# Output copies and x splits put in another order at block ends, and ten conversion steps put later, in a fused attention, ELU and gated kernel

## The chip, the cores and the metric

One core of a Trainium2 chip runs the whole program. Five engines work beside one another, each through its own queue in order: TensorE (PE in the profile; PEld is its weight load), VectorE (DVE), ScalarE (ACT), GpSimd (POOL) and the queue of SyncE (SP), which issues all DMAs of this kernel. The metric is the device time of one execution in microseconds; lower is better.

## What is computed

The reference is a chunked softmax attention whose output feeds two feed-forward layers, cut here to what matters:

```python
# q, k, v: (8, 8, 576, 64), chunks of 64
attn = softmax(q_c @ k_c.T / 8)             # per chunk, rows of 64
x = (attn @ v_c) as (4608, 512)             # tokens x model
h = x @ w_in                                # 512 -> 2048
x = where(h > 0, h, exp(min(h, 0)) - 1) @ w_out      # 2048 -> 512
gate = 1 / (1 + exp(-(x @ w_gate)))         # 512 -> 1536
out = (gate * (x @ w_val)) @ w_out2         # 1536 -> 512
```

## The kernel before, in words

**Precision.** Weights arrive as 64-bit floats and are turned into fp32 on the chip. Every large product is three matmuls in fp32r: each operand is cut into a high part (a cast) and a low part (the fp32 value minus the high part), and high x high, low x high and high x low are added (`PASSES`, lines 33 and 188). A low part of x or of the activations g is a subtraction on VectorE or, for some chunks of x, on GpSimd (`split`, lines 94 to 96; `split_x`, line 182). The profile shows all these subtractions under line 96 and the casts under line 90, except for block 0, where they stand at lines 423 and 664.

**Blocks and slots.** The 4608 tokens are nine blocks of 512. A block's first layer pair is 16 slots, one for each 128 of the 2048 inner columns. Slot s is number f = s mod 16 of block j = s div 16 and runs on TensorE, in this order: some attention work of the next block, `layer_1(s)` (12 matmuls into `h`, lines 425 to 431 and 189; the input x is four chunks of 128 rows, `xs0` to `xs3`, with one buffer each), and `layer_2(s-2)` (12 matmuls into four output banks `y0` to `y3`, line 441, again one buffer each). The ELU of a slot is spread over the next: ScalarE takes exp (`elu_exp`, line 405) and relu (408), VectorE one fused sum (`elu_sum`, 411), ScalarE the cast (`elu_split`), VectorE the low part (`elu_low`, 423; in later blocks line 96).

**Attention of later blocks.** Even slots start with the scores of a pair of chunks (line 280), odd slots with the product with v (`values`, line 379). From pair 10 on (slot 18), q and k are split in odd slots (lines 248 to 258), and the probabilities are turned by small DMAs (line 346) and split (lines 92, 96, 357) in the next even slot.

**Block ends.** Before slot f = 0 of a new block can run `layer_1`, its x chunks must be split; before slot f = 2 can run `layer_2` for the new block, the finished `y0` to `y3` must be copied out (`y_out`, lines 449 to 459: even banks by ScalarE, odd ones by VectorE, each into a tile of the pool `e`, then a DMA to memory).

**Block 0** has no block before it to hide its attention. `first_block` (lines 555 to 664) runs eight pairs through all engines; in its last rounds (the drain) it finishes x chunk by chunk. The weights of the first layer pair are converted at the same time: `convert` (line 106) makes a list of 162 small steps, five for each of 32 weight tiles: a sign, a clamp, an add, a shift and a subtraction on VectorE (lines 140, 134, 146, 137, 155), three of them with an operation on ScalarE beside it (a cast, line 90, and lines 128 and 124); the add also issues the DMA that loads a later tile (line 118). `bg(n)` puts the next n steps of the list at its place in the code. `PRE_STEPS` says how many each round of `first_block` takes, the other tables how many each slot takes.

The order on each engine is the order of the code (`manual_schedule`); waits follow from the data and the buffers.

Of the kernel before, what the change touches and what calls it, by code (L numbers as in the profile page):

```python
# [8 lines left out]
F32 = mybir.dt.float32  # L9
# [8 lines left out]
CH = 64  # L18
# [5 lines left out]
NB = NT // TB  # L24
# [15 lines left out]
EARLY, EARLY_LAG = 2, 5  # L40


PRE_STEPS = (0, 0, 3, 3, 2, 2, 2, 2, 2, 2, 4, 4, 4)
FIRST_STEPS, A0_STEPS, A8_STEPS, B_STEPS = 3, 9, 6, 9

W_AT = (1, 2, 4, 6)

# [5 lines left out]
def kernel(  # L53
# [27 lines left out]
    w_p = ctx.enter_context(tc.tile_pool(name="w", bufs=2 * F1))  # L81
    x_p = ctx.enter_context(tc.tile_pool(name="x", bufs=1))
    g_p = ctx.enter_context(tc.tile_pool(name="g", bufs=2))
    e_p = ctx.enter_context(tc.tile_pool(name="e", bufs=3))
    ps_y = ctx.enter_context(tc.tile_pool(name="ps_y", bufs=1, space=bass.MemoryType.PSUM))
    ps_h = ctx.enter_context(tc.tile_pool(name="ps_h", bufs=2, space=bass.MemoryType.PSUM))

# [94 lines left out]
    def split_x(key, kk, lo_eng):  # L182
        x = xs[key, kk] = x_p.tile([128, 2, TB], F32R, tag=f"xs{kk}", name=f"xs{kk}")
        split(xr.pop((key, kk)), x[:, 0], x[:, 1], nc.scalar, lo_eng)
# [18 lines left out]
    def phase_a():  # L203
        with (
# [87 lines left out]

            def first_parts(P, what):

                t = st[P, what + "1"] = s_p[0].tile([128, 4, CH], F32, tag="s1", name="s1", bufs=2)
                for a, p in enumerate(halves):
                    nc.scalar.copy(out=t[p], in_=parts_of(st[P, what], p, a)[0])  # L297

# [36 lines left out]

            def blocks_out(P):

                d = s_p[0].tile([128, 2, 4, 32], F32, tag="dt", name="dt", bufs=2)
                nc.vector.transpose(
                    out=d.rearrange("p b n q -> p n b q"),  # L340
                    in_=st.pop((P, "p")).rearrange("p n (b k) -> p n b k", b=2),
                )
                t = st[P, "tt"] = s_p[0].tile([64, 4, 128], F32, tag="tt", name="tt", bufs=2)
                for b in range(2):
                    for w in range(4):
                        nc.sync.dma_start(
                            out=t[32 * b:32 * b + 32, w],
                            in_=d[32 * w:32 * w + 32, b].rearrange("p n q -> p (n q)"),
                        )
# [99 lines left out]
            def y_out(j, es=range(KC)):  # L449
                for e in es:  # L450
                    if j == NB - 2:
                        y = xr_tile("y", e)
                    else:
                        y = e_p.tile([128, TB], F32, tag="e", name="y")
                    if e % 2 == 0:
                        nc.scalar.copy(out=y, in_=y_t.pop((j, e)))  # L456
                    else:
                        nc.vector.tensor_copy(out=y, in_=y_t.pop((j, e)))
                    nc.sync.dma_start(out=ymid[j][:, e], in_=y)

            def slot(s, steps=0):
# [9 lines left out]
                def is_pair(n, least=0):  # L471
                    return least <= n < NP
# [8 lines left out]
                else:  # L481
# [3 lines left out]
                        first_parts(V, "v")  # L485
                    elif is_pair(V):
                        values_out(V)
                if f == 0 and j > 0:
                    split_x(j, KC - 1, nc.vector)
                if s >= F1:  # L490
                    elu_sum(s - 1)
                if even and is_pair(P):
# [17 lines left out]
                    elu_sum(s - 1)  # L510
                if s >= EARLY:
                    layer_1(s, 2)
                if f == 2 and j > 0:
                    y_out(j - 1, (2, 3))
                if s == F1 - 1:

                    layer_1(s, 3)
                    transposes(T)
                    transposes_out(T)
                if last:  # L520
                    split_x(nxt, 0, nc.gpsimd)
                bg(q[1])
                layer_1(s)
                if s > 0:
                    elu_split(s - 1)
                if even and 0 <= P < P32:
                    softmax_exp(P)
                if last:
                    split_x(nxt, 1, nc.vector)
                now = not even and 0 <= T < P32 and s >= F1  # L530
                if now:
                    transposes(T)
                elu_exp(s)
                if now:
                    transposes_out(T)
                if even and PB <= P < P32:
# [2 lines left out]
                if 0 < s <= F1:  # L539
                    elu_low(s - 1)  # L540
                elu_rest(s)
                if last:
                    split_x(nxt, 2, nc.gpsimd)
                bg(q[3])
                if even and is_pair(P) and P < PB:
                    softmax_sum(P)
                if s >= 2:
                    layer_2(s - 2)
                if not even and is_pair(T) and s < F1 - 1:
                    transposes(T)  # L550
                    transposes_out(T)
                if f == 1 and j > 0:
                    y_out(j - 1, (0, 1))

            def first_block(load_w):

# [109 lines left out]
            with (  # L666
                tc.tile_pool(name="conv0", bufs=2) as conv_p,
                tc.tile_pool(name="ps_0", bufs=2, space=bass.MemoryType.PSUM) as ps_p[0],
            ):
                make_identity(nc, ident)  # L670
                tiles = [(k, w_src[k[0]][k[1]], w_p) for k in w1]
                first_block(convert(tiles, conv_p, len(W_AT), 6))
                for s in range(F1):
                    slot(s, A0_STEPS if s else FIRST_STEPS)
                bg(len(todo))
            with (
                tc.tile_pool(name="att2", bufs=1) as s_p[0],
# [7 lines left out]
    def phase_b(slot, layer_2, elu_sum, elu_split, y_out):  # L685
        with (
# [2 lines left out]
            tc.tile_pool(name="ps_b", bufs=2, space=bass.MemoryType.PSUM) as ps_b,  # L689
        ):  # L690
            tiles = [(k, w_src[k[0]][k[1]], w_p if n < 2 * F1 else w2_p) for n, k in enumerate(w2)]
            load_w = convert(tiles, conv_p, 4, 4)
            for n in range(4):
                load_w(n)
            for s in range((NB - 1) * F1, NB * F1):
                slot(s, A8_STEPS if s < NB * F1 - 1 else 0)
# [157 lines left out]
```

## Time and profile before

| | |
|---|---|
| three timed runs | 1807.86, 1809.66, 1810.4 us; median 1809.66 |
| the profiled execution | 1808.78 us, of which the span from the first to the last instruction is 1807.0 |
| TensorE busy | 1776.1 us (98%), mean granted clock 0.997 |
| VectorE, ScalarE, GpSimd busy | 1044.9 (58%), 757.1 (42%), 44.2 (2%) |

A busy TensorE is one with a matmul under way; matmuls overlap, so a steady stream shows no idle time. The timeline gives each group of equal instructions its start, its length and, in brackets, the idle time of its engine before it with the instruction that ended it. The span has three parts: block 0 with its attention (0 to some 141 us), the slots of blocks 1 to 8 (to some 918 us) and the gated layers.

### The profile page before, as it was taken

How to read it: one execution, taken by the hardware profiler on the slowest of the kernel's cores; microseconds unless marked ns; L12 is line 12 of the kernel's file. 1: busy time of each engine (PE TensorE's matmuls, PEld its weight loads, DVE VectorE, ACT ScalarE, POOL GpSimd, SP SyncE). 2: the span in 40 equal slices, each digit the busy share in tenths (PEclk: the TensorE clock that was granted, in tenths of full speed). 3: DMA queues.
4: the chain of work that ended last, by engine and by line, in shares of the span. 5: the costliest groups of instructions: out<-in, count | busy, mean ns of one | idle time of the engine just before them, and what ended most of it. 6: DMA issues, size and time to landing. Idle time of an engine off the chain costs nothing.

```text
span 1807.0 us, 21535 instructions
## 1 busy us (share of the span) xinstructions
PE 1776.1 (98%) x8068; PEld 1471.1 (81%) x8068; DVE 1044.9 (58%) x1980; ACT 757.1 (42%) x1411; POOL 44.2 (2%) x50
## 2 busy tenths in 40 slices
PE   7999999999999999999999999999999999999999
PEld 6887878788888878788888888888888888888887
DVE  7997888888888888887767423222222222222322
ACT  7775666767666766767654201010110101010101
POOL 1000000000000000000000000000000000000000
PEclk9999999999999999999999999999999999999999
DMA  6652121121212122215343101000010101010000
GB/s 231 200 169 77 57 80 59 58 69 53 74 57 82 48 79 59 69 47 166 117 128 106 47 1 47 1 24 24 9 38 0 47 0 48 1 47 1 24 1 24
DMA packets 61593, 111.52 MB, mean 62 GB/s; under 512 B 11056, under 2 KB 30000, under 8 KB 61488
## 3 DMA queue, kind: packets, MB, share of 16 engines
q1 hardware_dynamic: 61488, 110.14, 19.3%
q8 instruction: 63, 1.03, 0.2%
q14 instruction: 42, 0.34, 0.1%
HBM read 84.15 MB, written 18.87 MB: 57 GB/s over the span
## 4 chain that ended last, share of the span: by engine, by line
PE 83%; DVE 9%; ACT 5%; issue 1%; DMA 1%; SPq 0%; POOL 0%; DVEq 0%
PE o L730 16%; PE pv L189 16%; PE pg L189 16%; PE y L441 16%; PE h L189 15%; PE banks L379 1%; PE banks L280 1%; ACT pt L357 1%; DVE t L140 1%; DVE elu L411 1%; DVE s L310 1%; DVE w L155 1%; DVE xs L96 1%; DVE qv L258 1%; DVE t L146 1%
## 5 line engine op out<-in xcount | busy, mean ns | idle before, releaser
L189 PE MATMUL h<-xs,w 128*128 128x512 f32 x1728 | 426.3, 394 | 5.7 <-DVE xs L96 3.9
L441 PE MATMUL y<-g,w 128*128 128x512 f32 x1728 | 419.5, 391 | 8.3 <-ACT y L456 7.6
L719 DVE TENSOR_TENSOR sg<-pv,sg 128x512 f32<-128x512 f32 x108 | 74.6, 691 | 548.6 <-PE pv L189 545.6
L441 PEld LDWEIGHTS y<-g,w 128*128 128x128 f32 x1728 | 323.2, 188 | 80.2 <-ACT y L456 10.1
L189 PEld LDWEIGHTS h<-xs,w 128*128 128x128 f32 x1728 | 317.1, 189 | 69.0 <-DVE xs L96 6.4
L714 ACT ACTIVATE sg<-pg 128x512 f32<-128x512 f32 x108 | 64.5, 597 | 676.9 <-PE pg L189 676.6
L189 PE MATMUL pv<-xs,w 128*128 128x512 f32 x1296 | 311.3, 389 | 0.0
L189 PE MATMUL pg<-xs,w 128*128 128x512 f32 x1296 | 311.3, 389 | 0.0
L730 PE MATMUL o<-w,g 128*128 128x512 f32 x1296 | 311.1, 389 | 0.0
L189 PEld LDWEIGHTS pv<-xs,w 128*128 128x128 f32 x1296 | 243.2, 188 | 50.5
L189 PEld LDWEIGHTS pg<-xs,w 128*128 128x128 f32 x1296 | 243.2, 188 | 50.5
L730 PEld LDWEIGHTS o<-w,g 128*128 128x128 f32 x1296 | 243.2, 188 | 50.5
L411 DVE SCALAR_TENSOR_TENSOR elu<-h,elu 128x512 f32<-128x512 f32 x144 | 99.4, 690 | 65.5 <-ACT elu L408 64.2
L405 ACT ACTIVATE elu<-h 128x512 f32<-128x512 f32 x144 | 86.0, 597 | 53.6 <-PE h L189 25.6
L297 ACT COPY s<-banks 64x256 f32<-64x256 f32 x216 | 78.2, 362 | 67.5 <-PE banks L280 64.3
L90 ACT CAST g<-elu 128x512 fp32r<-128x512 f32 x144 | 89.3, 620 | 23.0 <-DVE elu L411 18.5
L408 ACT ACTIVATE elu<-elu 128x512 f32<-128x512 f32 x144 | 90.9, 631 | 3.8
L96 DVE TENSOR_TENSOR g<-elu,g 128x512 fp32r<-128x512 f32 x128 | 87.9, 686 | 6.3 <-ACT g L90 4.6
L96 DVE TENSOR_TENSOR g<-sg,g 128x512 fp32r<-128x512 f32 x108 | 74.9, 694 | 3.7
L96 POOL TENSOR_TENSOR xs<-xr,xs 128x512 fp32r<-128x512 f32 x26 | 36.8, 1417 | 1631.1 <-ACT xs L90 1631.1
L315 ACT ACTIVATE e<-s 128x256 f32<-128x256 f32 x64 | 26.8, 418 | 111.2 <-DVE s L312 110.7
L357 ACT CAST pt<-pt 64x512 fp32r<-64x512 f32 x108 | 66.8, 619 | 4.5 <-DVE pt L92 2.2
(86 smaller groups left out, 1299.2 us busy)
## 6 DMA issues: line engine op xcount, KB each, us to landing
raw<-in_qkv SPq DMA_DIRECT2D x54, 512.0 KB, 3.7
wraw<-in_w_out SPq DMA_DIRECT2D x28, 512.0 KB, 3.5
xr<-ymid SPq DMA_DIRECT2D x36, 256.0 KB, 3.6
wraw<-in_w_in SPq DMA_DIRECT2D x16, 512.0 KB, 3.7
ymid<-y SPq DMA_DIRECT2D x32, 256.0 KB, 3.1
out<-o SPq DMA_DIRECT2D x32, 256.0 KB, 2.0
tt<-dt SPq DMA_DIRECT2D x432, 16.0 KB, 1.8
wraw<-in_w_gate SPq DMA_DIRECT2D x12, 512.0 KB, 3.6
```

Source lines behind the costliest of these rows:

```text
L90: nc.scalar.copy(out=out, in_=raw)
L96: lo_eng.tensor_sub(out=lo, in0=raw, in1=hi)
L189: nc.tensor.matmul(out=ps, lhsT=w[:, zw, kk * 128:(kk + 1) * 128], rhs=xs[key, kk][:, zx], start=(kk == 0 and n == 0), stop=(kk == KC - 1 ...
L297: nc.scalar.copy(out=t[p], in_=parts_of(st[P, what], p, a)[0])
L357: nc.scalar.copy(out=t[h1, z], in_=t[h0, z])
L405: nc.scalar.activation(out=e_t[s], in_=h_t[s], func=ACTF.Exp)
L408: nc.scalar.activation(out=e_t[s], in_=e_t[s], func=ACTF.Relu, scale=-1.0, bias=1.0)
L411: nc.vector.scalar_tensor_tensor(out=e_t[s], in0=h_t.pop(s), scalar=0.0, in1=e_t[s], op0=ALU.max, op1=ALU.subtract,)
L441: nc.tensor.matmul(out=y_t[j, e], lhsT=w[:, zw, e * 128:(e + 1) * 128], rhs=g[:, zx], start=(f == 0 and n == 0), stop=(f == F1 - 1 and n = ...
L714: nc.scalar.activation(out=sg, in_=pg, func=ACTF.Sigmoid)
L719: nc.vector.tensor_tensor(out=sg, in0=pv, in1=sg, op=ALU.mult)
L730: nc.tensor.matmul(out=o_t[t], lhsT=g[:, zx, t * 128:(t + 1) * 128], rhs=w[:, zw], start=(f == 0 and n == 0), stop=(f == F2 - 1 and n == 2),)
```

## The change

It does the following.

- **Block ends, x.** All four chunks of the next block are split in the last slot of a block, right behind `layer_1`, the low parts all on VectorE. Before, chunk 0 stood ahead of the end of `layer_1` and chunk 2 behind the relu, both with the low part on GpSimd; chunk 1 stood behind the cast of the ELU and chunk 3 in the first slot of the next block, both on VectorE.
- **Block ends, y.** All four copies stand at the end of slot f = 1. Before, banks 0 and 1 stood there, banks 2 and 3 in slot f = 2.
- **Buffers.** The pool `e` has 5 buffers instead of 3; the tiles `s1`, `dt` and `tt` of the attention have one instead of two; in the second conversion three weight tiles are loaded ahead instead of four.
- **Conversion steps.** The rounds 8 to 12 of `first_block` take 8 steps instead of 16. Slot 0 takes 4 instead of 3, slot 1 takes 5 instead of 9, slots 2 to 15 take 10 instead of 9 until the 162 are done.
- **Pair 1's turned probabilities** move from the end of slot 1 into slot 2, behind `layer_1`.

```diff
-PRE_STEPS = (0, 0, 3, 3, 2, 2, 2, 2, 2, 2, 4, 4, 4)
-FIRST_STEPS, A0_STEPS, A8_STEPS, B_STEPS = 3, 9, 6, 9
+PRE_STEPS = (0, 0, 3, 3, 2, 2, 2, 2, 1, 1, 2, 2, 2)
+FIRST_STEPS, A0_STEPS, A8_STEPS, B_STEPS = 4, 10, 6, 9
...
-    e_p = ctx.enter_context(tc.tile_pool(name="e", bufs=3))
+    e_p = ctx.enter_context(tc.tile_pool(name="e", bufs=5))
...
-                if f == 0 and j > 0:
-                    split_x(j, KC - 1, nc.vector)
                 if s >= F1:
                     elu_sum(s - 1)
...
                 if s >= EARLY:
                     layer_1(s, 2)
-                if f == 2 and j > 0:
-                    y_out(j - 1, (2, 3))
...
-                if last:
-                    split_x(nxt, 0, nc.gpsimd)
                 bg(q[1])
                 layer_1(s)
+                if last:
+                    for kk in range(KC if j + 1 < NB else KC - 1):
+                        split_x(nxt, kk, nc.vector)
+                if s == 2:
+                    transposes(1)
                 if s > 0:
                     elu_split(s - 1)
                 if even and 0 <= P < P32:
                     softmax_exp(P)
-                if last:
-                    split_x(nxt, 1, nc.vector)
...
                 elu_exp(s)
+                if s == 2:
+                    transposes_out(1)
...
                 elu_rest(s)
-                if last:
-                    split_x(nxt, 2, nc.gpsimd)
                 bg(q[3])
...
-                if not even and is_pair(T) and s < F1 - 1:
+                if not even and is_pair(T) and 1 < s < F1 - 1:
...
                 if f == 1 and j > 0:
-                    y_out(j - 1, (0, 1))
+                    y_out(j - 1)
...
-                    slot(s, A0_STEPS if s else FIRST_STEPS)
+                    slot(s, FIRST_STEPS + s if s < 2 else A0_STEPS)
...
-            load_w = convert(tiles, conv_p, 4, 4)
-            for n in range(4):
+            load_w = convert(tiles, conv_p, 3, 4)
+            for n in range(3):
                 load_w(n)
```

**ScalarE in slot 31, the last of block 1** (`xs0` to `xs3` are block 2's x, `g` and `elu` the ELU of slots 30 and 31). Before:

```order
L255 CAST qv_2402<-raw_2321 64x2x256
L90 CAST xs0_2415<-xr0_1557 128x512
L90 CAST g_2424<-elu_2375 128x512
L90 CAST xs1_2427<-xr1_1807 128x512
L405 ACTIVATE elu_2430<-h_2408 128x512
L408 ACTIVATE elu_2430<-elu_2430 128x512
L90 CAST xs2_2433<-xr2_2044 128x512
L297 COPY s1_2454<-banks_1499 64x256 x2
L90 CAST xs3_2457<-xr3_2281 128x512
```

Now:

```order
L255 CAST qv_2402<-raw_2321 64x2x256
L90 CAST xs0_2421<-xr0_1557 128x512
L90 CAST xs1_2424<-xr1_1807 128x512
L90 CAST xs2_2427<-xr2_2044 128x512
L90 CAST xs3_2430<-xr3_2281 128x512
L90 CAST g_2433<-elu_2375 128x512
L405 ACTIVATE elu_2436<-h_2408 128x512
L408 ACTIVATE elu_2436<-elu_2436 128x512
```

The four high parts stand together ahead of the ELU's cast, exp and relu; on VectorE the four low parts stand together in the same way, between line 258 and the ELU's low part.

**VectorE over the end of slot 33 and slot 34** (`y1` and `y3` are finished banks of block 1; the rows from line 310 to 339 are the softmax of a pair, `g` the ELU's low parts). Before:

```order
L458 COPY y_2573<-y1_1668 128x512
L411 SCALAR_TENSOR_TENSOR elu_2555<-h_2539,elu_2555 128x512
L310 TENSOR_TENSOR s_2586<-banks_1499,s1_2582 64x256 x2
L311 TENSOR_REDUCE m_2587<-s_2586 128x4
L312 TENSOR_TENSOR s_2586<-s_2586,m_2587 128x256
L92 CAST pt_2593<-tt_2480 64x512
L96 TENSOR_TENSOR pt_2593<-tt_2480,pt_2593 64x512
L319 TENSOR_REDUCE d_2598<-e4_93 128x4
L320 RECIPROCAL d_2598<-d_2598 128x4
L322 TENSOR_TENSOR p_2601<-e4_93,d_2598 128x256
L339 STREAM_TRANSPOSE dt_2603<-p_2601 128x4x2x32
L458 COPY y_2624<-y3_1670 128x512
```

Now:

```order
L96 TENSOR_TENSOR g_2552<-elu_2505,g_2552 128x512
L458 COPY y_2573<-y1_1668 128x512
L458 COPY y_2579<-y3_1670 128x512
L411 SCALAR_TENSOR_TENSOR elu_2555<-h_2539,elu_2555 128x512
L310 TENSOR_TENSOR s_2592<-banks_1502,s1_2588 64x256 x2
```

The copy of `y3` moved from behind the softmax of slot 34 to ahead of it; on ScalarE the copy of `y2` moved likewise, from behind lines 315 and 357.

**ScalarE in the last rounds of block 0's drain** (`w`, `wraw` and `t` from `wraw` are conversion steps; `xs3` is the last chunk of block 0's x). Before:

```order
L90 CAST xs2_389<-xr2_363 128x512
L90 CAST w_391<-t_234 128x512
L128 ACTIVATE wraw_211<-wraw_211 128x512
L648 COPY zeros_104<-ps_t_394 64x2x128 x2
L654 COPY xr3_419<-bank_397 64x256 x2
L124 ACTIVATE t_422<-wraw_271 128x512
L90 CAST w_436<-t_294 128x512
L128 ACTIVATE wraw_271<-wraw_271 128x512
L654 COPY xr3_419<-bank_427 64x256 x2
L90 CAST xs3_443<-xr3_419 128x512
```

Now:

```order
L124 ACTIVATE t_387<-wraw_211 128x512
L645 COPY zeros_104<-ps_t_390 64x2x128 x2
L651 COPY xr3_404<-bank_393 64x256 x2
L90 CAST w_407<-t_234 128x512
L128 ACTIVATE wraw_211<-wraw_211 128x512
L651 COPY xr3_404<-bank_411 64x256 x2
L90 CAST xs3_431<-xr3_404 128x512
```

Between the fourth last round and the high part of `xs3`, six conversion operations (one of them just ahead of the rows shown) became three.

## Rows read from the trace of the kernel before

**Rows 1.** The page, part 1: busy time, share, instructions

```profile
PE 1776.1 (98%) x8068; PEld 1471.1 (81%) x8068; DVE 1044.9 (58%) x1980; ACT 757.1 (42%) x1411; POOL 44.2 (2%) x50
```

**Rows 2.** Waits, whole span: who waited for whom, us in total, times, longest

```profile
ACT elu L405 <- DMA ymid<-y: 15.2, 6, 2.7
...
PE y L441 <- ACT y L456: 7.6, 6, 1.3
...
PE h L189 <- DVE xs L96: 3.9, 6, 0.7
```

**Rows 3.** Timeline, TensorE, blocks 1 to 2: start, length, what [idle before <-releaser]

```profile
227.82 0.63 PE L280 MATMUL banks<-kz,qv 128*128 128x256 f32 x4
...
239.70 0.65 PE L280 MATMUL banks<-kz,qv 128*128 128x256 f32 x4
...
242.15 1.88 PE L189 MATMUL h<-xs,w 128*128 128x512 f32 x7 [0.64 <-DVE xs L96]
...
246.88 0.75 PE L379 MATMUL banks<-pt,qv 128*128 128x256 f32 x4
...
252.92 0.63 PE L280 MATMUL banks<-kz,qv 128*128 128x256 f32 x4
...
258.94 1.91 PE L441 MATMUL y<-g,w 128*128 128x512 f32 x6 [1.30 <-ACT y L456]
...
266.63 0.63 PE L280 MATMUL banks<-kz,qv 128*128 128x256 f32 x4
...
278.63 0.63 PE L280 MATMUL banks<-kz,qv 128*128 128x256 f32 x4
```

**Rows 4.** Timeline, the other engines, same stretch

```profile
236.65 0.62 ACT L90 CAST xs<-xr 128x512 fp32r<-128x512 f32 x1
...
237.41 1.71 POOL L96 TENSOR_TENSOR xs<-xr,xs 128x512 fp32r<-128x512 f32 x1 [92.71 <-ACT xs L90]
...
238.00 1.67 DVE L258 TENSOR_TENSOR qv<-raw,qv 64x512 fp32r<-64x512 f32 x1
...
240.31 2.38 DVE L96 TENSOR_TENSOR xs<-xr,xs 128x512 fp32r<-128x512 f32 x2
...
242.72 0.69 DVE L411 SCALAR_TENSOR_TENSOR elu<-h,elu 128x512 f32<-128x512 f32 x1
...
252.53 0.57 ACT L456 COPY y<-y 128x512 f32<-128x512 f32 x1
...
258.30 0.59 ACT L456 COPY y<-y 128x512 f32<-128x512 f32 x1
```

**Rows 5.** Windows, start of program: busy by engine, TensorE clock, DMA share, GB/s

```profile
35.00:40.00 5.00, 3.77 (x17) 2.60 (x15) 3.63 (x7) 4.87 (x11) 0.00 (x0) 1.00 0.35 105
...
45.00:50.00 5.00, 5.00 (x18) 3.94 (x18) 4.93 (x12) 4.55 (x10) 0.00 (x0) 0.50 0.77 247
```

**Rows 6.** Windows, VectorE alone, two slots of block 0

```profile
68.00:81.00 13.00, 12.90 (x28) 1.00 0.67 204
```

**Rows 7.** Timeline, block 0 and its end, all engines

```profile
40.14 0.62 ACT L90 CAST xs<-xr 128x512 fp32r<-128x512 f32 x1
...
42.30 0.69 DVE L664 TENSOR_TENSOR xs<-xr,xs 128x512 fp32r<-128x512 f32 x1
...
50.25 0.69 DVE L423 TENSOR_TENSOR g<-elu,g 128x512 fp32r<-128x512 f32 x1
...
136.51 0.69 DVE L423 TENSOR_TENSOR g<-elu,g 128x512 fp32r<-128x512 f32 x1
...
138.41 2.90 PE L441 MATMUL y<-g,w 128*128 128x512 f32 x12
...
144.75 1.19 PE L189 MATMUL h<-xs,w 128*128 128x512 f32 x4 [0.62 <-POOL xs L96]
...
145.77 2.90 PE L441 MATMUL y<-g,w 128*128 128x512 f32 x12
...
161.24 0.96 PE L441 MATMUL y<-g,w 128*128 128x512 f32 x3 [0.66 <-DVE y L458]
```

More of the change, by code (lines that the diff above doesn't have):

```diff
@@ L293, in first_parts @@
             def first_parts(P, what):
-                t = st[P, what + "1"] = s_p[0].tile([128, 4, CH], F32, tag="s1", name="s1", bufs=2)
+                t = st[P, what + "1"] = s_p[0].tile([128, 4, CH], F32, tag="s1", name="s1")
                 for a, p in enumerate(halves):
@@ L336, in blocks_out @@
             def blocks_out(P):
-                d = s_p[0].tile([128, 2, 4, 32], F32, tag="dt", name="dt", bufs=2)
+                d = s_p[0].tile([128, 2, 4, 32], F32, tag="dt", name="dt")
                 nc.vector.transpose(
@@ L342, in blocks_out @@
                 )
-                t = st[P, "tt"] = s_p[0].tile([64, 4, 128], F32, tag="tt", name="tt", bufs=2)
+                t = st[P, "tt"] = s_p[0].tile([64, 4, 128], F32, tag="tt", name="tt")
                 for b in range(2):
```

## The prediction

> **What bounds the kernel now.** I read the page's busy times first: TensorE is busy 1776.1 of 1807.0 us [rows 1], so no more than some 31 us of waiting can go. About 11 of these lie in the first 45 us, where block 0 has nothing to overlap with; the table of waits tells where the rest is. TensorE waits six times for a low part of x on VectorE and six times for a copy of a finished output bank on ScalarE [rows 2]: once each at six block ends. The timeline of one of them gives the true price, since matmuls overlap and the bracket understates a stop. The score matmuls of even slots are a clock that strikes every two slots: 227.82 to 239.70 is an undisturbed stretch, 11.88 us; the next three take 13.22, 13.71 and 12.00 [rows 3]. So one block end costs 1.34 + 1.83 + 0.12 = 3.29 us, and the six from block 1 to block 7 cost 19.7. The end of block 0 is a seventh, with its own waits (0.62 and 0.66 in brackets [rows 7]); after block 7 TensorE does not stop.
>
> Block 0's slots are the other place to read. There VectorE is busy 12.90 of the 13 us that two slots take [rows 6], and TensorE never stops either: two engines at their limit at once. The low part of slot 13's ELU ends at 136.51 + 0.69 = 137.20, and the matmuls that need it start at 138.41 [rows 7]. VectorE is only 1.2 us ahead.
>
> **The x splits at a block end.** The first stop has a cause that the timeline shows. GpSimd's subtraction runs from 237.41 for 1.71 us, and beside it line 258 on VectorE takes 1.67 us; two chunks of x, beside GpSimd's next one, take 2.38 [rows 4], where one operation of that length alone takes 0.69 (the ELU's sum at 242.72 [rows 4]). So GpSimd costs VectorE about 0.98 + 1.0 us, and chunk 1, caught behind it, is what the matmul at 242.15 waited for [rows 3]. The Trainium skill, "SBUF — State Buffer", section "Who interferes with whom", calls this an exclusive lock for two-input VectorE operations against a reading GpSimd operation; line 258 ends 0.55 us after GpSimd, which fits a blocked start better than a slow run. By that rule alone up to both GpSimd operations, some 3.1 us, would return to VectorE instead of 2.0, and the wait of 0.35 us left below would go too, 2 us over six ends.
>
> Now all four low parts are VectorE's. In slot 31 ScalarE begins the high parts at 236.65 as before [rows 4]; four at 0.62 end near 239.1, the last not held up, since `layer_1(31)` is through chunk 3 about 237. Line 258 starts at 238.00 and, alone, ends at 238.7; four low parts at no more than 0.69 end by 241.4. TensorE has its scores at 239.70 [rows 3] and starts `layer_1(32)` half a microsecond later; a matmul takes (11.88 - 1.0)/48 = 0.227 us (48 in two slots, beside 1.0 us of attention), so chunk 3's low part, for the twelfth matmul, is wanted at 240.2 + 11 x 0.227 = 242.7. It is there. What is late next: behind the four on VectorE stand the ELU's low part (to 242.0, wanted by `layer_2(30)` at 242.9) and the ELU's sum, which starts near 241.9 instead of 242.72. The softmax and the split probabilities hang on that sum; before, they let `values` start at 246.88 [rows 3], now 0.85 earlier, at 246.0. TensorE comes there at 240.2 + 24 x 0.227 = 245.65. It waits 0.35, and the stretch takes 12.35 us instead of 13.22.
>
> **The y copies.** Before, `y2` is copied at 258.30, behind the softmax of slot 34 [rows 4], and the matmuls into that bank start at 258.94 after 1.30 us of idleness [rows 3]. Now it follows `y0`, whose copy ran at 252.53 [rows 4], 0.87 earlier by the shift above: `y0` 251.7, `y2` 252.3, on VectorE `y1` 252.5 and `y3` to 253.9. `layer_2(32)` now wants them at 252.05 + 0.47 + 2.73 = 255.25, so 1.4 us of room hide them. The five buffers make four copies at once possible. Two things are queued behind: VectorE's sum, softmax and split probabilities of slot 34 are 0.6 later by one copy and 0.87 earlier by the shift, ready at 257.9 for a TensorE at 258.0; and the split of q and k in slot 35, which I place at 263.8, against scores wanted at 263.9. Both just make it, so the stretch takes 11.9 instead of 13.71. On SP the next raw load stands behind four output DMAs, so it issues near 255 for a use at 260, with several microseconds of DMA between. The next stretch loses its 0.12, since exp no longer waits for an output DMA (15.2 us in six waits on ScalarE [rows 2]).
>
> Sum for one end: 38.93 us of three stretches become 12.35 + 11.9 + 11.88 = 36.13, **2.8 us saved, 16.8 for six**. Bounds: all of the 3.29 (19.7), or only the y part, 1.95 (11.7), if VectorE's longer row costs at `values` or at the scores what it saves at x.
>
> **The moved conversion steps.** In the drain ScalarE is the limit: from 35 to 40 us it is busy 4.87 of 5, VectorE 3.63 [rows 5]. Three of its conversion operations, at about 0.6, now stand behind the high part of chunk 3, not ahead (40.14 [rows 7]), so this comes at 38.4; the low part, which at 42.30 [rows 7] stood behind steps that waited for ScalarE, follows at 39.0, **3.3 us earlier**. By the queue order, slot 0's ELU then has its low part at about 47.0 instead of 50.25 [rows 7]. It has ten steps fewer ahead of it; at 0.49 us each (28 instructions in 13 us are 0.46, and steps are three long and two short in five; an estimate from [rows 6]) that is 4.9 us of work gone for 3.25 us gained, so VectorE idles 1.6 us more in the drain. The steps are not gone: up to slot 13's low part there are 129 behind that point instead of 117. VectorE was full over that way (136.51 - 50.25 = 86.26 us [rows 7]) and needs 12 x 0.49 = 5.9 more. It gets there at 47.0 + 86.26 + 5.9 = 139.1, and TensorE's `layer_2(13)` starts at 139.85, not 138.41: **1.4 us later**, the head start eaten by waits for VectorE over the slots. Loads move with their add steps, by at most a slot on a lightly used SP; the weights themselves are ready a slot ahead of their use.
>
> At the end of block 0 the four low parts follow in time, so the way from `layer_2(13)` to `layer_2(14)`, 145.77 - 138.41 = 7.36 us with the stop at 144.75 [rows 7], becomes 6.27: 146.1, 0.35 later. The wait for a y copy at 161.24 [rows 7] goes, with what it cost, 0.9. Block 0 and its end: **0.5 us saved**. Bounds: 5 saved, if VectorE does not bind; 2 lost, if each moved step costs 0.6 and the drain idles more.
>
> The smaller buffers and pair 1's moved transposes I take at nothing: each reader is ahead of the next writer on the same engine or a slot away. Three weight tiles ahead instead of four leaves a load six steps of time; it is covered by the slack of the gated slots, where TensorE never waits.
>
> The profiled execution: 1808.78 - 16.8 - 0.5 = **1791.5 us**. It lies 0.9 below the median of the runs, within their spread.
>
> **Rivals.** (1) *VectorE's longer row at a block end moves the stop.* For it: my margins at `values` and at the scores are 0.1 us or negative. Against: GpSimd's interference goes. Then 1.95 per end: 1808.8 - 11.7 - 0.5 = 1796.6. (2) *VectorE does not bind in block 0*, its steps packing closer than 0.49: the 3.3 us stay, with both stops at the block end, so 5: 1808.8 - 16.8 - 5 = 1787. Against it: 12.90 of 13. (3) *Slower: TensorE's clock falls in block 0.* Before, it was granted 0.50 from 45 to 50 us, after a drain in which TensorE was busy 3.77 of 5 us [rows 5]. Ten steps a slot make TensorE wait up to 0.6 us in each slot, and at half clock a slot's 24 matmuls take 5.5 us more; even with VectorE's 0.6 hidden in that, four such slots cost 4 x 4.9 = 19.6 us and eat all gain (1811); from there on it is slower, eight give 1831. Against: around the block ends, with waits of that size, the profile's clock row shows full speed. The Trainium skill, "TensorE: Matmul & The Clock Gate", section "What's actually happening", says that throttled is the default state and activity releases it, which is the rule against thinning out TensorE's work here; no row of block 0's slots shows it. (4) *The order does not do what it says*: a wait that I take to end at the copies ends elsewhere, and nothing moves, 1808.
>
> **How the numbers follow.** Forecast 0.65 (its own range 1789 to 1794.5), rival 1 0.15, rival 2 0.11, rival 3 0.05, rival 4 0.04. The range takes in rivals 1 and 2: 1786.5 to 1798. About 0.2% (3.6 us) is what a measurement here can tell from no change; forecast and rivals 1 and 2 are beyond it: faster 0.91, same 0.04, slower 0.05.
>
> **What would show it.** Stretches between the scores of slots 32, 34, 36 near 12.35 and 11.9; no wait of `y` for line 456; line 258 at 0.69. In block 0, the last low part of x near 39 us, TensorE stopping before matmuls that need the ELU from about slot 6 on, and `layer_2(13)` near 140. Wrong would be a stop at the scores of slot 36, a start of `layer_2(13)` before 137, or a low clock after 60 us.

## The result and the profile after

Three timed runs of the changed kernel gave 1791.81, 1793.2 and 1794.21 us, median **1793.2**, against 1809.66: a ratio of 0.991, 95% interval [0.9888, 0.9933]. It is faster by 16.5 us. The profiled execution took 1791.81 us, its span 1789.9 (1808.78 and 1807.0 before).

Busy times and two groups of matmuls on the page (busy, mean ns of one | idle time before them and what ended it), to be held against [rows 1]:

```profile
PE 1768.4 (99%) x8068; PEld 1469.8 (82%) x8068; DVE 1040.0 (58%) x1998; ACT 758.9 (42%) x1411; POOL 17.5 (1%) x32
...
L189 PE MATMUL h<-xs,w 128*128 128x512 f32 x1728 | 422.2, 393 | 3.0 <-DVE elu L411 3.0
L441 PE MATMUL y<-g,w 128*128 128x512 f32 x1728 | 416.4, 390 | 0.3 <-DVE g L423 0.3
```

The waits of the two groups, us in total, times, longest, against [rows 2]:

```profile
PE h L189 <- DVE elu L411: 3.0, 7, 0.9
...
PE banks L379 <- ACT pt L357: 1.8, 6, 0.6
```

No matmul waits for a low part of x or for a copied `y` any more. Three waits have come instead: `layer_1` for the ELU's sum, seven times, all in block 0 (in slot 2 and in slots 10 to 15); `values` for the split probabilities, once at each of six block ends; and, once, the scores of the next pair (line 266) for the load of its q and k. This last wait, 1.38 us at 43.45, is there because the lighter drain reaches the matmul before a load issued at 39.77 has landed; the kernel before has none at that place. The wait of exp for an output DMA, 15.2 us [rows 2], is not in the table any more.

TensorE at the end of block 1, against [rows 3] (start, length, what, [idle before]; line numbers are 3 lower than before from the middle of the file on):

```profile
238.41 0.63 PE L280 MATMUL banks<-kz,qv 128*128 128x256 f32 x4
...
244.73 0.75 PE L379 MATMUL banks<-pt,qv 128*128 128x256 f32 x4 [0.23 <-ACT pt L357]
...
250.82 0.63 PE L280 MATMUL banks<-kz,qv 128*128 128x256 f32 x4
...
262.75 0.63 PE L280 MATMUL banks<-kz,qv 128*128 128x256 f32 x4
...
274.63 0.63 PE L280 MATMUL banks<-kz,qv 128*128 128x256 f32 x4
```

The three stretches are 12.41, 11.93 and 11.88 us, 36.22 in place of 38.93. VectorE and ScalarE there, against [rows 4]:

```profile
236.72 0.69 DVE L258 TENSOR_TENSOR qv<-raw,qv 64x512 fp32r<-64x512 f32 x1
237.44 2.50 DVE L96 TENSOR_TENSOR xs<-xr,xs 128x512 fp32r<-128x512 f32 x4
...
240.57 0.69 DVE L411 SCALAR_TENSOR_TENSOR elu<-h,elu 128x512 f32<-128x512 f32 x1
...
250.38 1.06 ACT L456 COPY y<-y 128x512 f32<-128x512 f32 x2
...
251.35 1.29 DVE L458 COPY y<-y 128x512 f32<-128x512 f32 x2
```

Line 258 is down from 1.67 to 0.69, four low parts of x take 2.50 together, and the copies stand in pairs, the last done at 252.64. Block 0, against [rows 7]:

```profile
30.80 1.13 PE L607 MATMUL bank<-zeros,qkv 128*128 128x256 f32 x4 [1.72 <-ACT xr L651]
...
38.17 0.69 DVE L661 TENSOR_TENSOR xs<-xr,xs 128x512 fp32r<-128x512 f32 x1 [1.31 <-ACT xs L90]
...
43.45 1.08 PE L266 MATMUL bank<-raw 128*128 128x64 f32 x8 [1.38 <-DMA raw<-in_qkv]
...
46.19 0.69 DVE L423 TENSOR_TENSOR g<-elu,g 128x512 fp32r<-128x512 f32 x1
...
99.75 3.02 PE L189 MATMUL h<-xs,w 128*128 128x512 f32 x12 [0.34 <-DVE elu L411]
...
134.91 2.38 PE L189 MATMUL h<-xs,w 128*128 128x512 f32 x9 [0.36 <-DVE elu L411]
...
138.64 0.69 DVE L423 TENSOR_TENSOR g<-elu,g 128x512 fp32r<-128x512 f32 x1
...
139.38 2.57 PE L441 MATMUL y<-g,w 128*128 128x512 f32 x10 [0.27 <-DVE g L423]
...
145.41 2.89 PE L441 MATMUL y<-g,w 128*128 128x512 f32 x12
```

VectorE alone in 13 us of these slots, against [rows 6]:

```profile
94.00:107.00 13.00, 12.90 (x28) 1.00 0.60 186
```

It is as full as before, with TensorE waiting for it now.

**A marker for comparing executions.** The first row is a matmul in the first block that stops 1.71 to 1.74 us in every kernel here. It does not come at the same time: at 31.75 in the profile of before, 30.80 in this one, 32.79 in `ends_sum` below, because the first matmuls of the program wait for loads of q, k and v of changing length. So times in block 0 are counted from this marker. From it to the scores of slot 20, past the end of block 0, were 136.67 us before and are 136.33 now. From there to the scores of slot 124, over all six block ends, 636.99 us became 621.68. The gated layers did not move. The span's 17.1 us are then 0.95 at the program's start, 0.34 in block 0, 15.31 at the six ends and 0.50 behind the last matmul, where the output DMAs land.

### The profile page after: what moved, and what is told of

Read it like the earlier page. It is cut to its first block, busy times and chain, and to the rows that moved or that the text cites. A ratio compares the mean times of both kernels' runs of the same rounds, so it can differ in the third digit from the quotient of the medians.

```text
span 1789.9 us, 21622 instructions
## 1 busy us (share of the span) xinstructions
PE 1768.4 (99%) x8068; PEld 1469.8 (82%) x8068; DVE 1040.0 (58%) x1998; ACT 758.9 (42%) x1411; POOL 17.5 (1%) x32
## 4 chain that ended last, share of the span: by engine, by line
PE 87%; DVE 8%; ACT 3%; issue 1%; DMA 0%; SPq 0%; DVEq 0%
PE y L441 17%; PE h L189 17%; PE o L727 16%; PE pv L189 16%; PE pg L189 16%; PE banks L379 1%; PE banks L280 1%; DVE t L146 1%; DVE t L140 1%; ACT pt L357 1%; DVE w L155 1%; DVE xs L96 1%; DVE s L310 1%; DVE t L134 1%; DVE t L137 1%
## 5 line engine op out<-in xcount | busy, mean ns | idle before, releaser
L96 DVE TENSOR_TENSOR xs<-xr,xs 128x512 fp32r<-128x512 f32 x60 | 43.0, 761 | 46.1 <-ACT xs L90 45.9
```

The source lines that it names most:

```text
L96: lo_eng.tensor_sub(out=lo, in0=raw, in1=hi)
```

## The experiments

Each kernel's median, its ratio to the kernel before on the same chip with the 95% interval, and from its profile the two distances just named:

| kernel | us | ratio | marker to slot 20 | slot 20 to 124 |
|---|---|---|---|---|
| before | 1809.66 | | 136.67 | 636.99 |
| the change | 1793.2 | 0.991 [0.9888, 0.9933] | 136.33 | 621.68 |
| ends_only | 1791.1 | 0.9899 [0.9884, 0.9914] | 134.62 | 621.47 |
| steps_only | 1811.31 | 1.0013 [1.0003, 1.0022] | 139.82 | 637.69 |
| no_clamp | 1787.47 | 0.9882 [0.9868, 0.9897] | 131.63 | 621.24 |
| sum_later | 1790.49 | 0.9898 [0.9883, 0.9913] | 137.79 | 618.45 |
| y_undone | 1803.38 | 0.9969 [0.9957, 0.9982] | 137.24 | 631.25 |
| x_undone | 1798.59 | 0.9944 [0.9929, 0.9958] | 138.14 | 626.44 |
| x_pool | 1796.4 | 0.9931 [0.9917, 0.9946] | 136.26 | 625.70 |
| x_order_vec | 1796.68 | 0.9935 [0.992, 0.995] | 136.77 | 625.35 |
| e3 | 1817.57 | 1.0046 [1.0029, 1.0063] | 136.56 | 646.48 |
| ends_sum | 1787.11 | 0.988 [0.9865, 0.9895] | 134.58 | 618.14 |
| clamp_pool_sum | 1784.84 | 0.9868 [0.9853, 0.9882] | 133.58 | 618.14 |
| ends_sum_clamp | 1787.4 | 0.9881 [0.9864, 0.9897] | 135.56 | 618.41 |

### The two halves of the change apart

`ends_only` is the changed kernel with the conversion steps and pair 1's probabilities where they were; `steps_only` is the kernel before with only those moved.

```diff
 ends_only, against the changed kernel
-PRE_STEPS = (0, 0, 3, 3, 2, 2, 2, 2, 1, 1, 2, 2, 2)
-FIRST_STEPS, A0_STEPS, A8_STEPS, B_STEPS = 4, 10, 6, 9
+PRE_STEPS = (0, 0, 3, 3, 2, 2, 2, 2, 2, 2, 4, 4, 4)
+FIRST_STEPS, A0_STEPS, A8_STEPS, B_STEPS = 3, 9, 6, 9
```

> The changed kernel with the conversion steps and pair 1's transposes where they stood before: only the new order at block ends and the buffers are left. Theory (VectorE binds block 0, so the lighter drain brings nothing by the end of the block): layer_2(13) starts near 138.4 as before, layer_2(14) near 144.7, the scores of slot 20 near 166.4 us (before 168.42, the whole change 167.13), and the time is 0.7 us under that of the whole change, 1791 to 1793. Rival (the lighter drain brings the 1.3 us that the whole change gained up to slot 20): scores of slot 20 near 168.4, time about 1794.5.

> The kernel before with only the moved conversion steps and pair 1's transposes. Theory: the last low part of block 0's x about 3 us earlier, TensorE stopping for VectorE in the later slots of block 0, layer_2(13) at 138.5 to 139.5, scores of slot 20 at 168.5 to 169.5 (before 168.42); time 1809 to 1811, not below the kernel before. Rival: the scores of slot 20 near 167.1 and 1.3 us less time, 1808.3.

The order at block ends is the whole gain: alone it gives 1791.1 us, 18 less than before, of which 2.05 lie at the end of block 0 and 15.5 at the six others. The moved steps alone make the kernel slower, by 2.5 us in medians (1811.31 against 1808.78 on that chip), an interval just above 1. In block 0 of `ends_only` TensorE does not wait for the ELU once; in `steps_only` it does, in slot 2 and in each slot from slot 10 on. The last two of these slots:

```profile
130.68 3.06 PE L189 MATMUL h<-xs,w 128*128 128x512 f32 x12 [0.37 <-DVE elu L411]
137.62 2.32 PE L189 MATMUL h<-xs,w 128*128 128x512 f32 x9 [0.32 <-DVE elu L411]
140.25 0.41 PE L328 MATMUL bank<-ident,p 128*128 128x128 f32 x2 [0.31 <-DVE p L322]
...
142.09 2.58 PE L441 MATMUL y<-g,w 128*128 128x512 f32 x10 [0.27 <-DVE g L423]
```

### Does VectorE bind block 0?

The changed kernel without the clamp in the first conversion, so with one VectorE operation in five less there and nothing else changed:

```diff
+            if not clamped:
+                return
...
-                first_block(convert(tiles, conv_p, len(W_AT), 6))
+                first_block(convert(tiles, conv_p, len(W_AT), 6, False))
```

> The changed kernel without the clamp of weight magnitudes in the first conversion (left out of the computation): one short VectorE operation in every five steps goes, about 0.34 us each, 0.7 per slot of block 0; ScalarE, the DMAs and the order stay. Theory (VectorE binds the slots of block 0): the stops of TensorE before layer_1 from slot 8 on go, layer_2(13) starts at 134 to 135.5 instead of 138.5, the time falls by 3.5 to 5 us to 1788 to 1790. Rival (ScalarE or the weights' arrival binds): the stops stay within 1 us of what they were, time 1792 to 1794.

All waits for the ELU from slot 3 on are gone (one in slot 2 stays, 0.65), and the way to slot 20 is 131.63 us: 4.7 less than the change, and 3.0 less than `ends_only`. The time, 1787.47 us, lies half a microsecond below what was expected. So VectorE binds block 0's slots: with room on it the stops go. That the 3.0 is the head start which the lighter drain gives (3.1 us at the low part of slot 0's ELU, counted from the marker) fits, but the old steps without the clamp were not run; `ends_sum_clamp` below, where the clamp only changes its engine, gains nothing with the old steps.

### The parts of the block ends

`y_undone` puts the copies of `y2` and `y3` back into slot f = 2, with five buffers in `e`; `e3` keeps the new order but takes the five buffers back to three.

```diff
 y_undone
+                if f == 2 and j > 0:
+                    y_out(j - 1, (2, 3))
...
-                    y_out(j - 1)
+                    y_out(j - 1, (0, 1))
 e3
-    e_p = ctx.enter_context(tc.tile_pool(name="e", bufs=5))
+    e_p = ctx.enter_context(tc.tile_pool(name="e", bufs=3))
```

> The changed kernel with the copies of y2 and y3 back in slot f = 2, all else kept, the five buffers too. My theory: the place of the copies makes the second stop, since ScalarE reaches y2 only behind the softmax; the second stretch goes back from 11.93 to about 13.7 with a wait of some 1.3 us at line 441, 1.8 us for each of six ends, 0.9 at block 0's end: 1793.2 + 10.8 + 0.9 = 1805 us (1802 to 1806). Rival: it was the three buffers that held the copies back; then the five buffers keep the stretch near 12.0 and the time at 1793 to 1794.

> The changed kernel with three buffers in the pool e again instead of five. Theory 1, the buffers are a needed part of the change: four copies in one slot and the ELU's tiles then ask for more tiles than there are, so the third and fourth copy wait for the output DMAs of the first two, some 2 to 2.5 us, with the copy of the scores behind them on ScalarE and the softmax of slot 34 behind those; the second stretch becomes 14 us or more, 2 us for each of six ends: 1805 us or more (to 1810), no better than the kernel before. Theory 2, there is room enough in the slots: 1793 to 1794.5 us, second stretch 11.9.

The stop for `y2` is back with the old place, and the second stretch is 266.42 - 252.79 = 13.63 us. TensorE in `y_undone`:

```profile
252.79 0.63 PE L280 MATMUL banks<-kz,qv 128*128 128x256 f32 x4
...
258.68 1.93 PE L441 MATMUL y<-g,w 128*128 128x512 f32 x6 [1.16 <-ACT y L456]
...
266.42 0.63 PE L280 MATMUL banks<-kz,qv 128*128 128x256 f32 x4
```

With three buffers the second stretch is 16.32 us (252.60 to 268.92), far worse than with the old order, and the kernel is slower than before. At 1817.57 us it also lies beyond the 1810 that was the most expected: a wait of 2 to 2.5 us was foreseen, and the stretch grew by 4.4. ScalarE, VectorE and TensorE in `e3`:

```profile
255.24 0.59 ACT L456 COPY y<-y 128x512 f32<-128x512 f32 x1 [2.47 <-DMA ymid<-y]
255.72 0.74 ACT L297 COPY s<-banks 64x256 f32<-64x256 f32 x2
...
256.54 0.69 DVE L458 COPY y<-y 128x512 f32<-128x512 f32 x1 [2.60 <-DMA ymid<-y]
...
261.26 1.01 PE L379 MATMUL banks<-pt,qv 128*128 128x256 f32 x4 [2.58 <-ACT pt L357]
```

The third and fourth copy wait for output DMAs, the copy of the scores stands behind one, the ELU's sum behind the other, and `values` of slot 35 pays. So the buffers are a condition of the new place: without them it costs more than the old.

For x, `x_undone` puts all four splits back, places and engines. `x_pool` and `x_order_vec` part place from engine: new place with chunks 0 and 2 on GpSimd, and old places with VectorE alone.

```diff
 x_pool
-                        split_x(nxt, kk, nc.vector)
+                        split_x(nxt, kk, nc.gpsimd if kk % 2 == 0 else nc.vector)
```

> The changed kernel with the four splits of x back at their old places and engines (chunks 0 and 2 on GpSimd), the copies of y at their new places. My theory: the first stretch goes back from 12.41 to 13.2 with a stop before line 189, the second stays near 11.9, since the copies of y have 1.4 us of room: 0.8 for each of six ends and some 0.9 at the end of block 0, 1793.2 + 4.8 + 0.9 = 1799 us (1797 to 1800). Rival: the two parts lean on each other, and without the earlier x the softmax and copies of y come late as well: second stretch 12.5 or more, 1803 or more. Other rival: the copies of y were all, first stretch 12.4, 1793.

> The changed kernel with the four splits together at their new place, but the low parts of chunks 0 and 2 on GpSimd again. It parts the place of the splits from their engine. If a subtraction of GpSimd holds up VectorE by 0.98 us as in the kernel before, VectorE's row takes 2 x 0.63 + 2 x 0.98 = 3.2 us instead of 2.50, the ELU's sum and the probabilities come 0.7 later and the first stretch is 13.1: 1793.2 + 6 x 0.7 = 1797.5 us. If it is held up for the whole of both subtractions, as the Trainium skill, SBUF - State Buffer, section Who interferes with whom, has it, 2 x 1.71 come to it and the stretch is 14: 1804. Rival: GpSimd takes load off VectorE without harm; VectorE's row takes 1.3, the stop of 0.23 at line 379 goes and the first stretch is 11.9: 1790.5 us.

> The changed kernel with the four splits of x back at their old places, but all low parts on VectorE. With the run that kept the new place and put GpSimd back (first stretch 13.10) it parts place from engine the other way round. Theory 1, the place costs by itself: chunk 3's high part stands on ScalarE behind the copy of the scores, so it ends 2.1 us after the scores begin (244.26 - 242.20 in the run with the old places), its low part at about 2.8, and the ELU's sum starts there instead of 2.16 behind the scores: the stop before line 379 grows by 0.6, the first stretch is 13.0, and the time 1793.2 + 6 x 0.6 = 1797 us (1796 to 1799), so that each of the two parts alone gains next to nothing. Theory 2, GpSimd was all of the cost: the first stretch stays near 12.4, 1793.5 us.

First stretches: 13.23 us with both undone, 13.10 with GpSimd back, 13.05 with the old places back, against 12.41. Each half alone is worth next to nothing, and the two do not add; both are needed. With GpSimd back the stop stands at `values`, not at x. GpSimd, VectorE and TensorE in `x_pool`:

```profile
235.90 0.68 DVE L257 TENSOR_TENSOR qv<-raw,qv 64x512 fp32r<-64x512 f32 x1
236.62 1.68 DVE L258 TENSOR_TENSOR qv<-raw,qv 64x512 fp32r<-64x512 f32 x1
238.32 2.27 DVE L96 TENSOR_TENSOR xs<-xr,xs 128x512 fp32r<-128x512 f32 x2
...
236.04 3.41 POOL L96 TENSOR_TENSOR xs<-xr,xs 128x512 fp32r<-128x512 f32 x2 [92.64 <-ACT xs L90]
...
1000.50 1.29 POOL L96 TENSOR_TENSOR xs<-xr,xs 128x512 fp32r<-128x512 f32 x1 [98.28 <-ACT xs L90]
...
245.38 0.75 PE L379 MATMUL banks<-pt,qv 128*128 128x256 f32 x4 [0.72 <-ACT pt L357]
```

With the old places and no GpSimd the cause is another one: chunk 3's cast stands on ScalarE behind the copy of the scores, the low part behind the cast, the ELU's sum behind the low part. ScalarE, VectorE and TensorE in `x_order_vec`:

```profile
240.75 0.75 ACT L297 COPY s<-banks 64x256 f32<-64x256 f32 x2 [0.23 <-PE banks L280]
241.51 0.62 ACT L90 CAST xs<-xr 128x512 fp32r<-128x512 f32 x1
...
242.17 0.69 DVE L96 TENSOR_TENSOR xs<-xr,xs 128x512 fp32r<-128x512 f32 x1 [0.56 <-ACT xs L90]
242.89 0.69 DVE L411 SCALAR_TENSOR_TENSOR elu<-h,elu 128x512 f32<-128x512 f32 x1
...
247.05 0.74 PE L379 MATMUL banks<-pt,qv 128*128 128x256 f32 x4 [0.86 <-ACT pt L357]
```

Taken out of the change one at a time, the x part is worth 626.44 - 621.68 = 4.8 us over the six ends and the copies 631.25 - 621.68 = 9.6. If the two add, some 1.0 of the 15.31 is neither; three buffers in the kernel before are the candidate, not measured by itself.

### The stop that is left, and the best version

`sum_later` is the changed kernel with VectorE's ELU sum of slot f = 0 moved behind the first part of the softmax and the split probabilities, in the blocks whose attention runs there.

```diff
-                if s >= F1:
+                if s >= F1 and (f or not is_pair(P - 1, P32)):
                     elu_sum(s - 1)
...
                     transposes_split(P - 1)
+                    if f == 0:
+                        elu_sum(s - 1)
```

> The changed kernel with one VectorE instruction moved: in the first slot of blocks 2 to 7 the ELU's sum stands behind the split of the probabilities, not ahead of the softmax. Theory (the stop of 0.35 us left at each block end is VectorE's row of four low parts, the ELU's low part and the sum ahead of the split probabilities): the stop before the product with v goes, the first stretch of a block end takes 12.0 to 12.1 instead of 12.41 us, 2 us less time, about 1791. Rival (the stop moves to the scores of the next even slot or to layer_1): the second stretch grows by what the first loses, 1793.

The stretches are 11.90, 11.91 and 11.88 us: the stop before `values` is gone, 3.2 us over six ends. Its block 0 was 1.5 longer, so the median gains only 2.7; the last section tells why. `ends_sum` is the same edit on `ends_only`.

> The new order at block ends with the old conversion steps, and the ELU's sum of the block's first slot put behind the split of the probabilities. If the moved steps cost what the run of the ends alone against the whole change said (0.7 by the medians, 1.7 by the way through block 0) and the later sum gives back 0.53 us at each of six ends (stretch 12.41 to 11.90), the two add up: 1791.1 - 3.2 = 1788 us (1787 to 1789.5), the three stretches at 11.9, 11.9 and 11.9, no stop in block 0's slots. Rival: they don't add, since with the later sum the probabilities of slot 34 or its softmax come late and the second stretch grows: 1791, with a stop at line 379 or 280 of the second stretch.

The two parts add: 1787.11 us. Last, the clamp of the first conversion on GpSimd instead of VectorE, on `sum_later` (`clamp_pool_sum`) and on `ends_sum` (`ends_sum_clamp`):

```diff
-            nc.vector.tensor_scalar(out=t, in0=t, scalar1=LEAST, ...
+            clamp_eng.tensor_scalar(out=t, in0=t, scalar1=LEAST, ...
```

> The changed kernel with the ELU's sum of a block's first slot later (as in the earlier run, 1790.5 us) and the clamp of the first conversion on GpSimd instead of VectorE. The run without the clamp gave 5.7 us in the profiled execution less than the whole change; this asks whether GpSimd can do that work beside VectorE. Theory 1, the clamp, which reads one tensor, runs on GpSimd in no more than a step's room and holds VectorE up by less than it takes off: no stops before line 189 in block 0's slots, 1785.5 to 1787 us. Theory 2, GpSimd's operation holds up the two-input operations of VectorE as its subtraction did at a block end (0.98 us each), 32 times: the slots of block 0 get longer by 0.3 us for each of 2.6 steps a slot, stops of 1 us and more, 1800 us or more. Theory 3, GpSimd itself takes several microseconds for one clamp and the conversion falls behind: waits of line 189 for w, well over 1800.

> The run ends_sum (new order at block ends, old conversion steps, later sum: 1787.1 us, slot 20's scores 134.58 us behind the marker matmul in the first block) with the first conversion's clamp on GpSimd. Together with the run of the moved steps and the clamp on GpSimd (1784.8 us, 133.58) it tells whether that gain is the clamp's or needs the moved steps. Theory 1, the moved steps are worth something only when VectorE has room, and room alone is worth little where TensorE doesn't stop in block 0's slots: with the old steps the clamp on GpSimd changes only the drain, where ScalarE is the limit: 134.6 (134.0 to 135.0), 1787 us (1786 to 1788). Theory 2, the clamp on GpSimd is the whole gain and the moved steps are worth nothing either way: 133.6 or less, 1785 us or less. Theory 3, GpSimd's 2.1 us for a clamp delay the conversion in the drain, where slots are not there to hide it: 136 or more, 1788.5 us or more.

`clamp_pool_sum` took **1784.84 us**, the least of all kernels here, 24 us below the kernel before and 8 below the change. A clamp takes 2.12 us on GpSimd (67.7 us for 32) instead of 0.42, but no matmul waits for VectorE in block 0's slots but one, in slot 2 (1.15). The time is a little under the 1785.5 to 1787 that were expected. GpSimd and VectorE in it:

```profile
75.28 4.28 POOL L134 TENSOR_SCALAR t<-t 128x512 f32<-128x512 f32 x2 [2.00 <-DVE t L146]
...
76.27 0.68 DVE L155 TENSOR_TENSOR w<-t,w 128x512 fp32r<-128x512 f32 x1
76.87 0.69 DVE L140 SCALAR_TENSOR_TENSOR t<-wraw,t 128x512 uint32<-128x512 uint32 x1
```

With the old steps the same edit gives nothing (1787.4 against 1787.11). Its way to slot 20, 135.56, lies half a microsecond above what was expected of "only the drain changes" and a microsecond above `ends_sum`. Some 0.6 of that stand in the drain: VectorE waits 2.1 us there for a clamp on GpSimd, the last low part of x comes 11.11 instead of 10.54 us behind the marker, and TensorE's stop for it is 1.80 instead of 1.26; the rest stays open. So moving the steps pays only where VectorE has room: with the clamp on VectorE it costs 1.7 us or more; with the clamp on GpSimd it brings 2.0 on the way to slot 20 and 2.6 in the medians.

## Why the prediction was right, step by step

**The six block ends** were right in kind and a little high in size: 2.8 us each, 16.8 in all, were predicted; 2.71 were saved at the first and 2.3 to 2.6 at the others, 15.31 in all. Of the 1.5 that are missing, 0.5 is the multiplication by six: the third stretch was 12.00 only at the first end (11.93 at the fifth, 11.88 at the others), so five ends cost 3.15 to 3.22 before instead of 3.29. The other 1.0 is what an end still costs: 0.57 to 0.63 at five of them and 0.94 at the sixth, where 0.49 was predicted (36.13 against 3 x 11.88). At the sixth, `values` waits 0.58 us, not 0.23, and VectorE idles ahead of the cast of the turned probabilities:

```profile
721.42 0.42 DVE L92 CAST pt<-tt 64x512 fp32r<-64x512 f32 x1 [0.29 <-issue]
```

The small DMAs bring what this cast reads. That one of them landed late is likely, not shown.

**The x splits.** Line 258 at 0.69, the four low parts in a row and the ELU's sum near where it was placed: all as predicted. The stop left at `values` cost 12.41 - 11.88 = 0.53, not 0.47. But the reason given for the first stop, GpSimd's interference, was only half of it. `x_order_vec` shows that the old places cost as much without any GpSimd: the matmul waited for whatever came last, and a second thing stood right behind the first.

**The y copies.** 11.93 for a predicted 11.9, and `y_undone` takes it back to 13.63. The two margins of 0.1 us (softmax of slot 34, scores of slot 36) held. "Five buffers make four copies at once possible" was told in passing; `e3` shows it to be a condition: without it a block end takes 4.1 us more than in the change ((646.48 - 621.68)/6) and 1.6 more than before, not 2.5 less.

**The moved steps.** Counted from the marker (0.95 us earlier in this execution), the last low part of x comes at 39.12 (39.0 predicted), slot 0's ELU low part at 47.14 (47.0), slot 13's at 139.59 (139.1), the first waiting matmul of `layer_2(13)` at 140.33 (139.85), `layer_2(14)` at 146.36 (146.1). So twelve more steps cost 6.2 us of VectorE's row, where 5.9 were taken. Apart from one stop in slot 2, TensorE began to stop at slot 10 (the row at 99.75), not at slot 6. Block 0 and its end: 0.34 saved, 0.5 predicted; by its parts 2.05 from the new order at its end (`ends_only`; the prediction's 1.1 and 0.9) and a loss of 1.7 from the steps (1.4). The smaller buffers and pair 1's transposes, taken at nothing, were not run by themselves; from slot 124 to the last group of matmuls both kernels take 991.57 us, so the three weight tiles ahead cost nothing.

**The sum** took 16.8 + 0.5 = 17.3 us from the profiled execution, and 15.31 + 0.34 = 15.65 came where it was placed. That 1791.5 met the measured 1791.81 so closely is owed to 1.45 us at the program's start and behind its last matmul, which differ from run to run and have nothing to do with the change. One reading was off, and no term goes by it: TensorE's waiting in the first 45 us is 13.0 (45.00 - 32.02 busy), not about 11.

**The rivals.** A moved stop (rival 1) is there, at `values`, but at 0.53 instead of 1.34; with GpSimd back it is 1.22 (`x_pool`), so it was close. That VectorE does not bind (rival 2) is refuted by `no_clamp`. A falling clock (rival 3): the granted clock was 1.00 from 50 us to the end of block 0, beside stops of 0.35 us in each slot from slot 10 on, though not in the drain, as the last section tells. That nothing moves (rival 4) is refuted by every row above.

## What to carry to other kernels

A stop names the input that came last, not the only late one. Before a fix is priced, look at what is next in the same row of waits: here place and engine of the x splits each hid behind the other, and new places of copies without buffers for them made the kernel slower than it was. A head start for one engine is worth only what the next full engine lets through; moving work into slots where an engine is busy 12.9 of 13 us gives the time back, and it became a gain when one conversion step in five left that engine.

## What the runs showed of the hardware

**Two-input subtractions on GpSimd and VectorE hold each other up.** In the rows of `x_pool`, line 258 takes 1.68 us beside GpSimd's first operation, where it takes 0.69 alone, and the two low parts 2.27, where four in a row take 2.50 in the changed kernel. So each operation on GpSimd costs VectorE 1.0 us. GpSimd's two take 3.41 together, where one by itself takes 1.29. The five operations behind line 257 last from 236.58 to 240.59, 4.0 us, where VectorE alone needs 0.69 + 2.50 = 3.2. Giving half of such work to GpSimd made the row longer. The rows fit operations that take turns: GpSimd's first, if it starts behind line 257, is done at 236.58 + 1.29 = 237.87, and line 258 ends 0.4 us after that. The Trainium skill, "SBUF — State Buffer", section "Who interferes with whom", has an exclusive lock there, and these rows agree; the 3.1 us by that rule in the prediction counted GpSimd's own waiting as VectorE's loss, which is 1.0 for each.

**A one-input operation on GpSimd holds VectorE up less, and not always.** Beside the clamp in the rows above, lines 155 and 140 took 0.68 and 0.69 us, as without it, though they read two operands and the clamp reads one. But two of VectorE's two-input operations in `clamp_pool_sum` and seven in `ends_sum_clamp` took 1.09 or 1.10 us instead of 0.69, and all nine began 0.2 to 0.6 us behind the start of a clamp (for one, line 155 at 45.11 behind a clamp at 44.90). The same section would let such a pair contend, since it asks only whether GpSimd's operation reads SBUF; these rows show it at the start of a clamp alone, 0.4 us at a time. GpSimd's own mean of 2.12 us, against 1.91 at the shortest, may be its side of it; that was not tried.

**The clock can fall in the drain, and not always at the same place.** The changed kernel and `sum_later` are the same up to block 1. Windows of the start of the change (span of the window, then busy time of TensorE, weight loads, VectorE, ScalarE and GpSimd, then granted clock, DMA share, GB/s):

```profile
30.00:35.00 5.00, 3.13 (x14) 2.39 (x15) 3.98 (x10) 4.80 (x12) 0.64 (x1) 1.00 0.21 84
35.00:40.00 5.00, 5.00 (x28) 4.29 (x28) 2.02 (x5) 4.11 (x10) 0.00 (x0) 1.00 0.34 105
40.00:45.00 5.00, 3.15 (x22) 2.47 (x20) 4.90 (x12) 4.28 (x9) 0.00 (x0) 0.99 0.53 165
45.00:50.00 5.00, 4.61 (x15) 3.72 (x16) 4.97 (x11) 3.98 (x7) 0.00 (x0) 0.67 0.74 228
```

And of `sum_later`:

```profile
25.00:30.00 5.00, 3.72 (x22) 2.88 (x20) 4.38 (x11) 4.84 (x12) 1.22 (x2) 1.00 0.25 81
30.00:35.00 5.00, 3.38 (x9) 2.62 (x10) 3.14 (x8) 3.88 (x11) 0.64 (x1) 0.56 0.37 109
35.00:40.00 5.00, 5.00 (x19) 4.08 (x18) 2.66 (x5) 4.19 (x11) 0.00 (x0) 0.76 0.33 105
...
45.00:50.00 5.00, 3.40 (x14) 2.81 (x15) 4.90 (x12) 3.93 (x9) 0.00 (x0) 0.77 0.65 178
```

In one the clock was at its lower level (1.2 GHz of 2.4) for part of 45 to 50 us, behind five microseconds in which TensorE was busy 3.15. In the other it was there for most of 30 to 40, behind five with 3.72, and again for part of 45 to 55. In `x_order_vec`, with the same drain, all windows from 25 to 55 us show 1.00. After 60 us no kernel shows less than full speed in block 0. A fall at 30 us delays the drain itself, which takes back part of the head start. It takes the four matmuls of the marker 2.07 us in `sum_later` and 1.13 in the change, and the last low part of x comes 8.95 us behind the marker in `sum_later`, `steps_only` and `clamp_pool_sum`, which all show the early fall, 8.17 behind it in `x_undone`, where the fall is shorter (0.79 and 0.86 in the two windows from 30 to 40), and 7.36 to 7.39 in the six kernels with the lighter drain whose clock stayed at 1.00 up to 40 us. The way to slot 20 is 137.79 us in `sum_later`, 136.33 in the change and 136.77 in `x_order_vec`: the early fall goes with the 1.5 us, and the late one with nothing that shows. It is also about half of the 3.15 us by which the way to slot 20 in `steps_only` is longer than before; the other half is near the 1.7 of the steps. No experiment set the clock. The Trainium skill, "TensorE: Matmul & The Clock Gate", section "What's actually happening", says that the number of slow matmuls at a kernel's start varies from run to run of the same kernel. Here it is the place of a fall in the drain that varies, between kernels that are alike up to there.
